# Split or unsplit key-value sums for two heads, a moved group of matmuls, and a split changed in one slot

## The chip, the cores and the metric

The kernel runs on one core of a Trainium2 chip. The metric is the device time of one launch in microseconds (us). Before the change three runs took 871.21, 871.63 and 871.66 us.

## What is computed

A linear attention, a mixture of experts with one expert per token, and a dense two-layer network, one behind the other, all in 32-bit floats:

```python
def phi(x):                                   # q, k, v: 4 batches x 8 heads x 576 tokens x 64
    proj = x @ w_phi                          # 64 -> 128
    proj = proj - max(abs(proj))              # of each row
    return concat([exp(proj), exp(-proj)])    # 256
kv, z = phi(k).T @ v, sum(phi(k))             # for each head
x = (phi(q) @ kv) / (phi(q) @ z + 1e-6)       # 2304 tokens x 512
e = argmax(normalised(x) @ normalised(expert_emb).T / tau)   # one of 8 experts
x = gate * (relu(x @ w1[e]) @ w2[e])          # 512 -> 1024 -> 512
h = x @ w_in                                  # 512 -> 2048
out = (h * sigmoid(h)) @ w_out                # 2048 -> 512
```

## The kernel before

**Split and unsplit products.** A float32 matrix product is made in one of two ways. Split: an operand is rounded to the faster fp32r format on ScalarE (`hi`), the remainder `lo` is subtracted on VectorE or GpSimd, and three matmuls (hi x hi, hi x lo, lo x hi) replace one. Unsplit: the float32 data go to TensorE as they are, in a slower form of matmul, and nothing need be rounded.

**The heads.** The loop over `g` from -2 to 31 (line 1478 and after) works at several heads at once. Within one pass, in the order of every engine's queue: `project(g + 3)` multiplies q and k of a head by w_phi on TensorE (line 402); `shift(g + 3)` takes the row maximum and subtracts it on VectorE (lines 411, 412; the second writes `d`); `kv_turn(g + 1)` turns the key-value sum (line 494, copied by VectorE in line 496); `numden(g)` makes numerators and denominators into the one tile `pnx` (lines 504, 509); `norm(g)` divides them on VectorE (lines 517 to 529); `qturn(g + 2)` transposes q (line 420); the exponentials of k of head g + 3 are taken on ScalarE; `kv_part(g + 2)` makes the key-value sum (line 481); `qexp(g + 2)` takes the exponentials of q; `high(g + 5)` and `low(g + 5)` round the next input z on ScalarE and subtract on GpSimd (lines 385, 391).

Where `g + 3 >= KWHOLE`, `kwhole` writes the two exponentials (line 445) and `kv_part` uses them unsplit with v. Otherwise `vhigh` and `vlow` split v (ScalarE line 424, GpSimd line 427), and `kexp`, `kround` and `klow` make each of the two exponentials (ScalarE line 437), round it (ScalarE line 449) and subtract (GpSimd line 453); `kv_part` then makes 15 fp32r matmuls. Before, KWHOLE is 26; heads 0 and 1 are unsplit too.

**The choice and the route.** Beside the heads VectorE converts packed weights of the last stage (`narrow`, lines 207 to 222, two steps in the passes of `BITS`). When a batch is done, `choose` picks each token's expert on VectorE (lines 534 to 555); for batch 2 all its steps are taken in the pass g = 24, in front of `norm(24)`. In the pass g = 25, `ranks` counts tokens per expert (lines 576 to 588 and 149 to 152). `route_first` is a generator that makes the token lists of the first six slots from batches 0 to 2; each `next(first)` takes a step. Its last step (lines 655 to 659) multiplies match matrices `bm` and `at` on TensorE into a free corner of the PSUM tile `pkv` of head 28, and VectorE copies and adds the result into the indices `gidx` and writes the expert registers `regs_a`. The tile tag of `pkv` has two buffers, so head 30 takes the buffer of head 28. Before, this last step stands in the pass g = 27, behind `kv_part(29)`, followed by `gather(0)` and `gather(1)`, which fetch the tokens of two slots with indirect DMAs from GpSimd (line 861). `load2(0)` on the SP queue reads `regs_a` in the pass g = 28. `xturn(0)` in the pass g = 29 transposes what `gather(0)` brought (line 901).

**The slots.** 22 slots of 128 tokens follow; slot s multiplies by w1 and w2 of its expert. `split(s, 2, i)` splits quarter i of w2 (lines 878 and 866, 1024 columns each; a quarter holds two half-blocks of 512). Of the last quarter `unsplit2(s)` half-blocks stay unsplit (line 893 instead of lines 826 to 828), and the matching part of the transposed activations is copied and not split (`halves`, lines 885 to 888). Before, two half-blocks are unsplit in slots 0 to 4 and one in slots 5 to 14 and 17.

The dense network follows in a form with seven products in place of eight; nothing of it is touched.

Of the kernel before, what the change touches and what calls it, by code (L numbers as in the profile page):

```python
# [20 lines left out]
B, H, S, D, F, E = 4, 8, 576, 64, 128, 8  # L21
# [18 lines left out]
HALF = (NSF - NP) // 2  # L40
POS = [2, 5, 1, 4, 0, 3] + [NP + i // 2 + HALF * (i % 2) for i in range(NSF - NP)]
SPLIT = NP + HALF
KWHOLE = 26
CA = 10
G = B * H
RK = 2
# [12 lines left out]


def unsplit2(s):
    return 2 if s < 5 else int(s < 15 or s == 17)

# [1 line left out]
def moe_kernel(ctx, tc, qk, v, w_phi, emb, tau, w1, w2, win, wout, out):  # L67
# [193 lines left out]
    def phase_all(ctx):  # L261
# [40 lines left out]
        def load_v(g):  # L302
            b, h = divmod(g, H)
            ve = ves[g % 4]
            nc.sync.dma_start(out=ve[:, 0:4, 0:64], in_=v[b, h, 0:512, :].rearrange("(c p) d -> p c d", p=P))
            nc.sync.dma_start(out=ve[others[1 - g % 2], 4, 0:64], in_=v[b, h, 512:S, :])
            st["v", g] = ve
# [86 lines left out]
        def whole(g):  # L394
            return g < 2 or g >= KWHOLE

# [8 lines left out]
        def shift(g, src=None):  # L405
            src = pqk if src is None else src
            n = chunks(g)
            pv = src[:, 0:n * 256].rearrange("p (n f) -> p n f", f=F)
            m = attA.tile([P, 2 * n], F32, name=f"m{n}")
            d = attA.tile([P, n, 2, F], F32, name=f"d{n}")  # L410
            nc.vector.tensor_reduce(out=m, in_=pv, axis=AX.X, op=ALU.max, apply_absolute_value=True)  # L411
            nc.vector.tensor_tensor(out=d.rearrange("p c s f -> p (c s) f"), in0=pv,  # L412
                                    in1=m.unsqueeze(2).to_broadcast([P, 2 * n, F]), op=ALU.subtract)
            st["d", g] = d
# [8 lines left out]
        def vhigh(g):  # L423
            nc.scalar.copy(out=vhs[g % 2][:, :, 0:64], in_=st["v", g][:, :, 0:64])

        def vlow(g):
            nc.gpsimd.tensor_tensor(out=vls[g % 2][:, :, 0:64], in0=st.pop(("v", g))[:, :, 0:64],
                                    in1=vhs[g % 2][:, :, 0:64].bitcast(F32), op=ALU.subtract)

        def kexp(g, s):  # L430
            kd = st["d", g][:, :, 1, :]
            n = chunks(g)
            if s == 0:
                st["k", g] = [pool.tile([P, n, 2, F], F32R, name=f"{nm}{n}", bufs=n - NB + 2)
                              for pool, nm in ((attA, "kl"), (attB, "kh"))]
            ke = attA.tile([P, NB, F], F32, name="ke", bufs=2)[:, 0:n]
            nc.scalar.activation(out=ke, in_=kd, func=AF.Exp, scale=1.0 - 2.0 * s)  # L437
            st["ke", g, s] = ke

        def kwhole(g):  # L440
            n = chunks(g)
            ke = attA.tile([P, n, 2, F], F32R, name=f"kl{n}", bufs=n - NB + 2).bitcast(F32)
            kd = st["d", g][:, :, 1, :]
            for s in range(2):
                nc.scalar.activation(out=ke[:, :, s, :], in_=kd, func=AF.Exp, scale=1.0 - 2.0 * s)
            st["k", g] = [ke]

        def kround(g, s):
            nc.scalar.copy(out=st["k", g][1][:, :, s, :], in_=st["ke", g, s])  # L449
# [142 lines left out]
        def matches(b):  # L592
            nc.vector.tensor_tensor(out=bm[:, b * NB:(b + 1) * NB], in0=jot.unsqueeze(1).to_broadcast([P, NB, P]),
                                    in1=lows.pop(b).unsqueeze(2).to_broadcast([P, NB, P]), op=ALU.is_equal)
# [262 lines left out]
        def gather(s):  # L857
            xg = mp.tile([P, DM], F32, tag="t2a", name="xg", bufs=3)
            n = (B - 1) * S if s < NP else NT
            p = POS[s]  # L860
            nc.gpsimd.indirect_dma_start(out=xg, out_offset=None, in_=xd[0:n, :],  # L861
                                         in_offset=bass.IndirectOffsetOnAxis(ap=gidx[:, p:p + 1], axis=0))
            st["xg", s] = xg
# [4 lines left out]
        def split(s, which, i, later=False):  # L868
            src = (raw1 if which == 1 else raw2)[s % 2].rearrange("p k f -> p (k f)")
            sl = src[:, i * 1024:(i + 1) * 1024]  # L870
            n = 1024
            if i == 3:
                n -= 1024 * unsplit1(s) if which == 1 else 512 * unsplit2(s)
            hi = lo = None
            if n:
                hi = wr.tile([P, 1024], F32R, tag=f"wh{which}", name=f"wh{which}", bufs=4)
                lo = wr.tile([P, 1024], F32R, tag=f"wl{which}", name=f"wl{which}", bufs=4)
                nc.scalar.copy(out=hi[:, 0:n], in_=sl[:, 0:n])  # L878
                if not later:
                    remainder(hi, lo, sl, n)  # L880
            st["w", which, s, i] = (hi, lo, sl, n)
            return lambda: remainder(hi, lo, sl, n)
# [14 lines left out]
        def xturn(s, early=False):  # L897
            xg = st.pop(("xg", s))
            pt = bank("xt", name="pxt")
            for k in range(4):  # L900
                nc.tensor.transpose(out=pt[:, k * P:(k + 1) * P], in_=xg[:, k * P:(k + 1) * P], identity=ident)  # L901
            xh = mp.tile([P, DM], F32R, name="xh")
            xl = mp.tile([P, DM], F32R, name="xl")
            xw = mp.tile([P, P], F32, name="xw")
            halves(pt, xh, xl, None if early else xw, DM - P * unsplit1(s))
            st["x", s] = (xh, xl, xw)
            return lambda: nc.scalar.copy(out=xw, in_=pt[:, DM - P:])
# [558 lines left out]
        first = None  # L1466
# [11 lines left out]
        for g in range(-2, G):  # L1478
# [11 lines left out]
            if g == G - H + 1:  # L1490
                first = route_first(r1)
# [2 lines left out]
                next(first)  # L1494
            if 2 <= g + 3 < G:
                shift(g + 3)
            if g == G - H + 2:
                next(first)
            if g == G - 1:
                xwhole = xturn(1, True)  # L1500
                wlast = split(1, 1, 2, True)
# [31 lines left out]
            if H <= g < G - H and h == RK:  # L1533
                ranks(b - 1, beside(g + 1))
                matches(b - 1)
            if KWHOLE <= g + 3 < G:
                kwhole(g + 3)
            if 3 <= g + 3 < KWHOLE:
                vhigh(g + 3)
                vlow(g + 3)  # L1540
            if 2 <= g + 3 < KWHOLE:
                kexp(g + 3, 0)
# [9 lines left out]
            for u in () if g == -2 else (3, 4) if g == -1 else (g + 5,):  # L1552
                if u < G:
                    load_v(u)
            if g == G - H + 3:
                next(first)
                gather(0)
                gather(1)
            if 2 <= g + 3 < KWHOLE:
                kround(g + 3, 1)  # L1560
                klow(g + 3, 1)
# [264 lines left out]
    with ExitStack() as c2:  # L1826
        phase_all(c2)
# [36 lines left out]
```

## Time and profile before

| | |
|---|---|
| profiled execution | 871.61 us |
| its span, first to last instruction | 870.0 us |
| mean granted clock of TensorE, share of full | 0.999 |
| TensorE (PE) busy | 857.8 us, 99% of the span |
| VectorE (DVE) busy | 703.1 us, 81% |
| ScalarE (ACT) busy | 609.7 us, 70% |
| GpSimd (POOL) busy | 269.2 us, 31% |

PE, DVE, ACT and POOL are the engines' names in the profile; PEld is TensorE's loading of the stationary operand, which overlaps PE; SP is the engine that issues most DMAs. A busy TensorE can still be one that waits in part of the time of a matmul, since ends of matmuls are modelled. Times in rows are in us from the start of the span, and "L402" is line 402 of the kernel.

### The profile page before, as it was taken

Reading aid. Unit: us, or ns where it says so; the run is one execution under the profiler, and the core shown is the slowest. Engines: PE = TensorE matmul, PEld = TensorE weight load, DVE = VectorE, ACT = ScalarE, POOL = GpSimd, SP = SyncE. Lnnn points to the kernel's source line nnn. Section 1 sums busy time; section 2 is a strip of 40 time slices with the busy share of each in tenths; the row PEclk is TensorE's granted clock in tenths of the full one; section 3 lists DMA queues with packets and bytes.
Section 4 is the critical chain, followed back from the end, with each engine's and each line's share of the span. In section 5 each row is a group of like instructions: output and inputs, shape, how many; then the busy total and the mean of one; then the engine's idle time right before and its main releaser. Section 6 shows DMA issues by size and latency. Waiting matters only on the chain. (4 is left out here: it accounts for less than half of the span.)

```text
span 870.0 us, 16082 instructions
## 1 busy us (share of the span) xinstructions
PE 857.8 (99%) x5730; PEld 786.8 (90%) x5730; DVE 703.1 (81%) x1112; ACT 609.7 (70%) x960; POOL 269.2 (31%) x261
## 2 busy tenths in 40 slices
PE   8999999999999999999999999999999999999996
PEld 6999999988777778888888899999999999999996
DVE  7888888897899999999998866666865797676762
ACT  6787888755977888888999866444546776556551
POOL 5888788721401533204220013032020101111011
PEclk9999999999999999999999999999999999999999
DMA  7445463439696696787599576588699944716221
GB/s 216 138 130 173 113 176 101 138 105 382 222 243 196 226 267 208 281 286 166 152 338 331 198 260 246 180 272 297 225 310 336 346 122 122 216 63 183 73 75 47
DMA packets 128805, 177.47 MB, mean 204 GB/s; under 512 B 26409, under 2 KB 89513, under 8 KB 128721
## 3 DMA queue, kind: packets, MB, share of 16 engines
q1 hardware_dynamic: 113888, 142.29, 50.4%
q0 software_dynamic: 14752, 34.09, 13.9%
q8 instruction: 46, 0.75, 0.4%
q14 instruction: 39, 0.31, 0.1%
q10 hardware_dynamic: 80, 0.03, 0.0%
HBM read 173.49 MB, written 55.18 MB: 263 GB/s over the span
## 5 line engine op out<-in xcount | busy, mean ns | idle before, releaser
L866 DVE TENSOR_TENSOR wl<-raw,wh 128x1024 fp32r<-128x1024 f32 (+1 forms) x166 | 190.1, 1184 | 16.9 <-ACT wh L878 11.0
L878 ACT CAST wh<-raw 128x1024 fp32r<-128x1024 f32 (+1 forms) x166 | 164.6, 1036 | 21.9 <-PE ph L828 7.4
L1137 ACT COPY ht<-puA 128x384 f32<-128x384 f32 x93 | 44.4, 479 | 79.3 <-PE puA L828 72.0
L453 POOL TENSOR_TENSOR kl<-ke,kh 128x640 fp32r<-128x640 f32 (+1 forms) x48 | 71.7, 1510 | 22.4 <-ACT kh L449 21.4
L826 PE MATMUL ph<-wh,xh 128*128 128x512 f32 x166 | 67.2, 405 | 0.0
L828 PE MATMUL ph<-wh,xl 128*128 128x512 f32 x166 | 65.1, 392 | 1.1 <-DVE xl L888 1.1
L827 PE MATMUL ph<-wl,xh 128*128 128x512 f32 x166 | 64.9, 391 | 0.0
L504 PE MATMUL pnx<-kv,qp 128*128 128x73 f32 x512 | 62.3, 275 | 0.0
L504 PEld LDWEIGHTS pnx<-kv,qp 128*128 128x128 f32 x512 | 59.9, 192 | 0.2
L411 DVE TENSOR_REDUCE m<-pqk 128x10 f32<-128x1280 f32 (+1 forms) x31 | 42.2, 1361 | 18.8 <-PE pqk L402 18.5
L402 PE MATMUL pqk<-wbd,zh 128*128 128x256 f32 x280 | 52.2, 285 | 0.5 <-DVE d L412 0.4
L437 ACT ACTIVATE ke<-d 128x640 f32<-128x640 f32 (+1 forms) x48 | 32.9, 685 | 26.9 <-DVE d L412 15.3
L861 POOL DMA_INDIRECT xg<-xd,gidx x22 | 29.5, 1343 | 70.9 <-PE pxt L901 30.0
L391 POOL TENSOR_TENSOR zl<-z,zh 128x640 fp32r<-128x640 f32 (+1 forms) x30 | 42.3, 1409 | 27.6 <-ACT zh L385 22.0
L1144 DVE TENSOR_TENSOR ht<-puC,ht 128x384 f32<-128x384 f32 x48 | 26.5, 553 | 30.0 <-PE puC L828 25.5
L402 PEld LDWEIGHTS pqk<-wbd,zh 128*128 128x128 f32 x280 | 43.1, 189 | 1.9 <-issue 1.2
L412 DVE TENSOR_TENSOR d<-pqk,m 128x1280 f32<-128x1280 f32 (+1 forms) x31 | 42.2, 1362 | 2.3 <-PE qt L420 1.2
L828 PE MATMUL pdA<-wod,hl 128*128 128x256 f32 x144 | 40.8, 284 | 0.0
L402 PE MATMUL pqk<-wbd,zl 128*128 128x256 f32 x140 | 39.4, 281 | 0.5 <-DVE zl L391 0.5
L828 PEld LDWEIGHTS ph<-wh,xl 128*128 128x128 f32 x166 | 31.2, 188 | 8.3 <-DVE xl L888 1.7
L1380 POOL DMA_INDIRECT out<-osd,oidx x10 | 12.9, 1289 | 81.6 <-ACT osd L1371 56.5
L461 ACT ACTIVATE qp<-qt 128x640 f32<-128x640 f32 (+1 forms) x64 | 37.8, 643 | 0.2 <-PE qt L420 0.2
(481 smaller groups left out, 2916.9 us busy)
## 6 DMA issues: line engine op xcount, KB each, us to landing
raw<-w SPq DMA_DIRECT2D x44, 1536.0 KB
raw<-w SPq DMA_DIRECT2D x44, 512.0 KB
hd<-ht SPq DMA_DIRECT2D x90, 192.0 KB
gb<-hd SPq DMA_DIRECT2D x18, 512.0 KB
ws<-wout SPq DMA_DIRECT2D x16, 512.0 KB
yd<-ys SPq DMA_DIRECT2D x22, 256.0 KB
z<-qk SPq DMA_DIRECT2D x16, 320.0 KB
raw<-win SPq DMA_DIRECT2D x10, 512.0 KB
```

Source lines behind the costliest of these rows:

```text
L391: eng.tensor_tensor(out=zl, in0=z, in1=zh.bitcast(F32), op=ALU.subtract)
L402: nc.tensor.matmul(out=to[:, c * 256:(c + 1) * 256], lhsT=z[:, c * P:(c + 1) * P], rhs=wbd[:, j].rearrange("p h f -> p (h f)"), start=(i = ...
L411: nc.vector.tensor_reduce(out=m, in_=pv, axis=AX.X, op=ALU.max, apply_absolute_value=True)
L412: nc.vector.tensor_tensor(out=d.rearrange("p c s f -> p (c s) f"), in0=pv, in1=m.unsqueeze(2).to_broadcast([P, 2 * n, F]), op=ALU.subtract)
L453: nc.gpsimd.tensor_tensor(out=kl[:, :, s, :], in0=st.pop(("ke", g, s)), in1=kh[:, :, s, :].bitcast(F32), op=ALU.subtract)
L504: nc.tensor.matmul(out=pn[:, c, 0:73], lhsT=qp[:, s, c * P:(c + 1) * P], rhs=kv[:, s, g % 2, 0:73], start=(s == 0), stop=(s == 1))
L826: nc.tensor.matmul(out=o, lhsT=ah, rhs=bh, start=first, stop=False, skip_group_check=more)
L827: nc.tensor.matmul(out=o, lhsT=ah, rhs=bl, start=False, stop=False, skip_group_check=more)
L828: return nc.tensor.matmul(out=o, lhsT=al, rhs=bh, start=False, stop=last, skip_group_check=more)
L866: nc.vector.tensor_tensor(out=lo[:, 0:n], in0=sl[:, 0:n], in1=hi[:, 0:n].bitcast(F32), op=ALU.subtract)
L878: nc.scalar.copy(out=hi[:, 0:n], in_=sl[:, 0:n])
L1137: nc.scalar.copy(out=htile(u, at), in_=BK[u, "A"])
```

## The change

Three edits. KWHOLE goes from 26 to 28, so heads 26 and 27 are split: in the passes g = 23 and 24 `vhigh`, `vlow`, `kexp`, `kround` and `klow` take the place of `kwhole`, and in the passes g = 24 and 25 `kv_part` has the split form. The last step of `route_first` and the two gathers move from the pass g = 27 to the pass g = 28, behind `project(31)` and `shift(31)`. And slot 5 has two unsplit half-blocks instead of one.

```diff
-KWHOLE = 26
+KWHOLE = 28
...
 def unsplit2(s):
-    return 2 if s < 5 else int(s < 15 or s == 17)
+    return 2 if s < 6 else int(s < 15 or s == 17)
...
             if 2 <= g + 3 < G:
                 shift(g + 3)
-            if g == G - H + 2:
+            if g in (G - H + 2, G - H + 4):
                 next(first)
+            if g == G - H + 4:
+                gather(0)
+                gather(1)
             if g == G - 1:
...
             for u in () if g == -2 else (3, 4) if g == -1 else (g + 5,):
                 if u < G:
                     load_v(u)
-            if g == G - H + 3:
-                next(first)
-                gather(0)
-                gather(1)
             if 2 <= g + 3 < KWHOLE:
```

G is 32 and H is 8, so G - H + 3 is 27 and G - H + 4 is 28.

## Rows read from the trace of the kernel before

**Rows 1.** The page, part 1: busy us, share of the span, instructions.

```profile
PE 857.8 (99%) x5730; PEld 786.8 (90%) x5730; DVE 703.1 (81%) x1112; ACT 609.7 (70%) x960; POOL 269.2 (31%) x261
```

**Rows 2.** The waits of VectorE, 172 to 208 us: total us, times, longest.

```profile
DVE m L411 <- PE pqk L402: 0.8, 1, 0.8
```

**Rows 3.** Timeline of TensorE: start us, us, engine, line, operation, out<-in, count.

```profile
170.01 0.36 PE L481 MATMUL pkv<-kh,vh 128*65 128x256 f32 x1
...
171.85 0.40 PE L402 MATMUL pqk<-wbd,zh 128*128 128x256 f32 x2
...
176.00 2.32 PE L481 MATMUL pkv<-kl,ve 128*65 128x256 f32 x10
177.97 0.58 PE L402 MATMUL pqk<-wbd,zh 128*128 128x256 f32 x2
...
180.63 1.95 PE L504 MATMUL pnx<-kv,qp 128*128 128x73 f32 x16
```

**Rows 4.** Timeline of VectorE, heads 25 and 27 and the pass g = 24.

```profile
162.12 1.22 DVE L412 TENSOR_TENSOR d<-pqk,m 128x1024 f32<-128x1024 f32 x1
...
164.44 1.27 DVE L222 SCALAR_TENSOR_TENSOR raw<-raw 128x512 int32<-128x512 int32 x1
...
174.73 1.22 DVE L412 TENSOR_TENSOR d<-pqk,m 128x1024 f32<-128x1024 f32 x1
...
178.82 0.69 DVE L222 SCALAR_TENSOR_TENSOR raw<-raw 128x512 int32<-128x512 int32 x1
...
179.94 0.42 DVE L522 TENSOR_TENSOR x<-pnx,rd 128x256 f32<-128x256 f32 x1
...
180.81 1.04 DVE L588 TENSOR_TENSOR rank<-rank,off 128x5 f32<-128x5 f32 x1
```

**Rows 5.** Timeline of GpSimd, the last split head and after.

```profile
165.12 2.97 POOL L453 TENSOR_TENSOR kl<-ke,kh 128x512 fp32r<-128x512 f32 x2
168.07 1.27 POOL L391 TENSOR_TENSOR zl<-z,zh 128x512 fp32r<-128x512 f32 x1
...
180.56 1.27 POOL L391 TENSOR_TENSOR zl<-z,zh 128x512 fp32r<-128x512 f32 x1 [4.93 <-ACT zh L385]
```

**Rows 6.** Timeline of all engines around the last projection, 197 to 211 us.

```profile
198.27 1.49 DVE L412 TENSOR_TENSOR d<-pqk,m 128x1280 f32<-128x1280 f32 x1
...
200.69 0.52 PE L655 MATMUL pkv<-at,bm 128*128 128x12 bf16 x15 [1.27 <-DVE at L650]
...
201.07 0.48 PE L402 MATMUL pqk<-wbd,zh 128*128 128x256 f32 x2
...
202.29 0.17 DVE L657 COPY pis<-pkv 128x12 f32<-128x12 f32 x1
...
202.77 1.23 DVE L411 TENSOR_REDUCE m<-pqk 128x8 f32<-128x1024 f32 x1
202.95 1.16 POOL L861 DMA_INDIRECT xg<-xd,gidx  x1 [7.15 <-DVE regs_a L659]
...
205.31 2.32 PE L481 MATMUL pkv<-kl,ve 128*65 128x256 f32 x10
...
210.15 0.60 PE L901 MATMUL pxt<-ident,xg 128*128 128x128 f32 x4
```

**Rows 7.** DMA issues of the whole span: operation, count, median us to landing.

```profile
xg<-xd,gidx POOLq DMA_INDIRECT x22, 5.6
```

**Rows 8.** Timeline of TensorE, end of slot 5's second product.

```profile
303.08 0.39 PE L826 MATMUL po<-wh,hh 128*128 128x512 f32 x1
...
303.76 1.02 PE L893 MATMUL po<-raw,hw 128*128 128x512 f32 x2
304.62 0.60 PE L934 MATMUL ht<-ident,hs 128*128 128x128 f32 x4
```

**Rows 9.** Timeline of TensorE, the first matmuls and a later group of the same.

```profile
1.27 3.95 PE L327 MATMUL qt<-ones 128*128 128x512 bf16 x10 [1.27 <-DVE ones L88]
...
9.31 1.69 PE L327 MATMUL pnx<-ones 128*128 128x512 bf16 x7
```

## The prediction

> **What bounds the kernel now.** I read the page's first part, then the waits of VectorE, then the timelines of the last heads, engine by engine. TensorE is busy for nearly the whole span [rows 1], so at first sight the only question is how much TensorE time the change removes. The waits of VectorE between 172 and 208 us tell another thing for the place where the change works: in these 36 us VectorE waited once, for 0.8 us, and that before 174 us [rows 2]. From then on it goes from one instruction to the next, because the choice of experts and the route are laid between the heads. TensorE and VectorE are both full there, and a delay of either is a delay of the end. After the heads the rest follows TensorE and ScalarE in a chain without slack, so I carry what is won or lost at the last heads to the end unchanged. The profiled execution took 871.61 us, 0.02 under the median of the three runs, so sums made in its rows need no correction.
>
> **Heads 26 and 27, TensorE.** The key-value sum of an unsplit head takes 1.97 us from its first matmul to the first of the projection behind it, that of a split head 1.84 [rows 3]. So the split saves 0.13 us a head, 0.26 for both, as an upper bound. It is worth nothing if VectorE sets the next step, and it does: the numerators of head 25 start at 180.63 [rows 3], right behind the normalisation of head 24, whose last part ends at 179.94 + 0.42 = 180.36 [rows 4], since both use the tile pnx. TensorE's margin over VectorE here is under 0.3 us. I count the saving as 0.
>
> **Heads 26 and 27, GpSimd against VectorE.** The split form adds for each head on ScalarE a rounding of v and two of the exponentials, and on GpSimd one subtraction for v and two for the exponentials. ScalarE has room; what its casts cost in delay is contained in the pattern that follows. Head 25, the last split one with an odd number, shows when GpSimd works: its shifted keys are ready at 162.12 + 1.22 = 163.34 [rows 4], its two key subtractions run from 165.12 to 168.09, and the subtraction of the next input z until 169.34 [rows 5]. That is 1.8 to 4.7 us and 4.7 to 6.0 us behind the keys. For head 27 the keys are ready at 174.73 + 1.22 = 175.95 [rows 4]. Laid behind them, the two key subtractions fill 177.7 to 180.7 and the one of z 180.7 to 182.0, where before GpSimd was idle until 180.56 [rows 5].
>
> In just this stretch VectorE has the choice of batch 2 (all nine steps at once, lines 534 to 555) and two bit operations (lines 220 and 222). What meets GpSimd is slow: line 222 takes 1.27 us at 164.44, where head 25's subtractions run beside it, and 0.69 at 178.82, where GpSimd is idle; and the 5-element operation of line 588 takes 1.04 us, ending with GpSimd's subtraction of z that began at 180.56 [rows 4, 5]. Such an operation, with two inputs in SBUF, ends only when GpSimd's does. Of the choice, lines 547 and 555 have this form. One meets the first key subtraction, the other the second, so line 555 ends at about 180.7. Line 220 follows in about the 0.69 of line 222, to 181.4, and line 222 meets the subtraction of z: 1.27 more, to 182.7. Before it ended at 178.82 + 0.69 = 179.51. **VectorE is 3.2 us later** at the normalisation of head 24, and TensorE, which waits for it, about 3.0 at the numerators of head 25. Then 0.87 comes back: line 588 no longer meets GpSimd and drops from 1.04 to about the 0.17 of another small operation [rows 6]. With VectorE full to the end of the heads [rows 2], 3.2 - 0.87 = 2.33 us remain. Bounds: nothing, if none of these operations meets GpSimd; and at most the two key subtractions and that of z waited for whole, 2.97 + 1.27 - 0.87 = 3.4. I take 2.33, because the same operations beside the same subtractions are in the trace.
>
> **The match products.** They leave TensorE's queue in front of the last projection, where they wait 1.27 us for line 650 [rows 6], and run behind it. The projection then starts when its bank is free, behind line 412 at 198.27 + 1.49 = 199.76, say at 199.9 instead of 201.07 [rows 6]: 1.2 us earlier. But little of this lasts. On VectorE the copy of the products (line 657) and the two operations behind it now stand behind the reduction and subtraction of head 31. These start at about 202.3 instead of 202.77, last 2 x 1.23, and end at 204.8; the copy of 0.17 ends at 204.97 [rows 6]. The products lie in the PSUM tile of head 28, and the key-value sum of head 30 takes that tile next. So this sum starts at about 205.05 instead of 205.31 [rows 6]: the gain shrinks to **0.26 us**. The upper bound is 1.27, if nothing else were late.
>
> Two gathers on GpSimd and the loads of the second weights on the SP queue stand behind the same indices and move by 204.8 - 202.3 = 2.5 us. The loads fill tiles that are first read after the last head; if that cover were gone they would cost up to 2.5. The gather of slot 0 was issued at 202.95, and its transposition started at 210.15 without a wait [rows 6]. Issued at 205.45 and wanted at 209.9, it has 4.4 us. The median landing of all gathers is 5.6 us [rows 7], so the wait is between 0 and 1.2 us; I take 0.2, as the DMA queues hold less at that time, the second weights not being asked for yet.
>
> **Slot 5.** One more half-block goes unsplit. An unsplit pair of matmuls takes 304.62 - 303.76 = 0.86 us, three split ones 303.76 - 303.08 = 0.68 [rows 8]: 0.18 us more on TensorE. ScalarE and VectorE lose a 512-column cast and subtraction. What that relieves is between 0 and the same 0.18; I take 0.
>
> **Sum:** 2.33 - 0.26 + 0.2 + 0.18 = +2.45 us, so 871.61 + 2.45 = **874.1 us**.
>
> **The rivals.** *Not slower: TensorE's account decides.* If GpSimd's subtractions fall between VectorE's operations instead of on them, VectorE is on time, and TensorE keeps 0.26 of the splits and between 0.26 and 1.27 of the match products, less 0.18: 870.3 to 871.3 us. For it speaks that VectorE's small operations take a small part of the stretch, and that GpSimd can only subtract what ScalarE has cast, so that a late cast leaves a gap for them; the point from which it decides is VectorE's margin of 0.3 us at the numerators of head 25. Against it speaks that GpSimd works through all of 177.7 to 182 without a hole. I give it 0.30, a third of that for a gain beyond 1.7 us with something freed in the slots.
>
> *Half of the collisions.* Line 222 starts before the subtraction of z, or line 555 before the second key subtraction, and the price falls by about 1.3 us: 872.8 us. Chance 0.20.
>
> *The clock falls.* TensorE would wait some 3 us in one place, more than twice the 1.27 of the trace [rows 6]. At the start, after idleness, ten matmuls of 512 columns took 3.95 us, 0.395 each; later seven took 1.69, 0.241 each [rows 9]: the levels of 1.2 and 2.4 GHz. One such start costs 10 x (0.395 - 0.241) = 1.5 us, so 875.6 us. The 1.27 us wait did not bring the clock down, as the mean granted clock of the span is nearly full (the table above), which says nothing of 3 us. The Trainium skill, "TensorE: Matmul & The Clock Gate", section on the HAM clock gate, says that the array's default is the lower clock and that idleness brings it back; by that rule the sum would be the 875.6 of this rival, by the rows it stays at 874.1. Chance 0.08.
>
> **The numbers.** The forecast itself has 0.42, with 873.4 to 875.2 as its own range. Changes under 0.2% (1.7 us) can hardly be told from none by a measurement of this kernel. Slower by more: the forecast and the clock, 0.50. Within: most of the first rival and the half collisions, 0.40. Faster: 0.10. The range of 8 in 10 takes in the first rival's lower end and the forecast's upper: 870.3 to 875.2.
>
> **What would show it.** In the changed trace: line 555 and line 222 of batch 2 ending with a GpSimd subtraction; a wait of 2.5 to 3.2 us of TensorE at line 504 for VectorE's normalisation; no wait at line 655; the key-value sum of head 30 starting with the end of line 657; the gather of slot 0 landing close to its transposition. I am wrong if the numerators of head 25 start within 0.5 us of 180.6, or if the last projection's 1.2 us are still there at the transposition of slot 0.

## The result, and the profile after

The changed kernel takes 879.11 us (median of five executions, 878.60 to 881.55) against 871.63: **7.5 us slower**, ratio 1.0083 with an interval of 1.0072 to 1.0094. The forecast was 874.1, the range ended at 875.2. The profiled execution after is the slowest of the five, 881.55 us with a span of 879.9, so its account ends 2.4 us above the median; where that lies is seen below.

The page's first part, changed kernel:

```profile
PE 862.2 (98%) x5739; PEld 790.6 (90%) x5739; DVE 704.4 (80%) x1111; ACT 612.7 (70%) x965; POOL 277.9 (32%) x267
```

TensorE is 4.4 us busier than in [rows 1], though the change gives it less to do at the heads. The waits of TensorE from 170 to 220 us (us in total, times, longest) say where to look:

```profile
PE pnx L504 <- DVE x L522: 2.3, 1, 2.3
PE pkv L611 <- DVE ohs L555: 0.6, 1, 0.6
PE pxt L901 <- DMA xg<-xd,gidx: 0.3, 1, 0.3
```

The wait at line 655 [rows 6] is gone, and a longer one stands at the numerators of head 25. The timeline of VectorE (start us, us, engine, line, operation) shows why the numerators wait; it answers to [rows 4]:

```profile
176.77 0.59 DVE L540 TENSOR_TENSOR lt<-lg,mx 128x40 f32<-128x40 f32 x1
...
177.64 0.20 DVE L545 TENSOR_REDUCE mx<-lt 128x5 f32<-128x40 f32 x1
177.87 0.96 DVE L547 TENSOR_TENSOR oh<-em8c,mx 128x40 bf16<-128x40 f32 x1
...
179.13 1.05 DVE L555 TENSOR_TENSOR ohs<-ohs 128x8 bf16<-128x8 bf16 x1
180.10 0.68 DVE L220 SCALAR_TENSOR_TENSOR raw<-raw 128x512 int32<-128x512 int32 x1
180.82 1.64 DVE L222 SCALAR_TENSOR_TENSOR raw<-raw 128x512 int32<-128x512 int32 x1
...
182.89 0.41 DVE L522 TENSOR_TENSOR x<-pnx,rd 128x256 f32<-128x256 f32 x1
...
183.67 0.16 DVE L588 TENSOR_TENSOR rank<-rank,off 128x5 f32<-128x5 f32 x1
```

The timeline of GpSimd over the same time answers to [rows 5]:

```profile
176.43 0.88 POOL L427 TENSOR_TENSOR vl<-ve,vh 128x320 fp32r<-128x320 f32 x1
177.41 2.75 POOL L453 TENSOR_TENSOR kl<-ke,kh 128x512 fp32r<-128x512 f32 x2
180.63 1.28 POOL L391 TENSOR_TENSOR zl<-z,zh 128x512 fp32r<-128x512 f32 x1 [0.46 <-PE pkv L582]
```

Lay the two side by side: line 540 ends with the subtraction of v, lines 547 and 555 with the first and the second key subtraction, each within 0.06 us. Line 555 works on 8 columns and takes 1.05 us. Line 222, of 512 columns, does not end with the subtraction of z but 0.55 us behind it (182.46 and 181.91). It did the same in the kernel before: what line 222 met at 164.44 [rows 4] was not a key subtraction but that of v, from GpSimd's timeline before:

```profile
163.83 1.34 POOL L427 TENSOR_TENSOR vl<-ve,vh 128x320 fp32r<-128x320 f32 x1
```

This one ended at 165.17, and line 222 at 165.71. The reduction of line 545 lies under the first key subtraction, too, and takes its 0.20 us all the same. The normalisation of head 24 ends at 183.30, 2.94 us later than before.

TensorE's timeline shows what the forecast had not counted; compare with [rows 3]:

```profile
180.23 0.17 PE L611 MATMUL pkv<-ohs,ones 128*128 128x8 bf16 x1 [0.60 <-DVE ohs L555]
...
183.35 3.69 PE L504 MATMUL pnx<-kv,qp 128*128 128x73 f32 x16 [2.27 <-DVE x L522]
...
190.99 0.40 PE L402 MATMUL pqk<-wbd,zh 128*128 128x256 f32 x2
```

The last row is the next projection, which in TensorE's timeline before starts here:

```profile
185.60 0.47 PE L402 MATMUL pqk<-wbd,zh 128*128 128x256 f32 x2
```

The numerators start 2.72 us late, and then the same 16 matmuls take 3.69 us where they took 1.95. From the numerators to the projection it is 7.64 us instead of 4.97. The windows of the changed kernel (stretch, length, busy us of PE, PEld, DVE, ACT and POOL, then the granted clock, the busy share of the DMA engines and GB/s) name the reason:

```profile
181.00:183.00 2.00, 0.08 (x1) 0.00 (x0) 1.93 (x5) 0.12 (x2) 0.91 (x1) 0.98 0.00 0
183.00:185.00 2.00, 1.65 (x8) 1.65 (x8) 1.83 (x9) 0.00 (x0) 0.00 (x0) 0.50 0.79 256
185.00:187.00 2.00, 2.00 (x11) 2.00 (x11) 1.97 (x2) 0.00 (x0) 0.00 (x0) 0.50 1.01 263
187.00:189.00 2.00, 2.00 (x11) 1.98 (x11) 1.43 (x6) 1.36 (x2) 0.00 (x0) 0.50 0.07 14
189.00:191.00 2.00, 2.00 (x16) 2.00 (x16) 0.86 (x5) 0.00 (x0) 0.00 (x0) 0.81 0.00 0
```

From 183 to nearly 190 us the granted clock is 0.50, the level of 1.2 GHz. TensorE is busy all that time, at half speed; this is where its busy time grew. The projection starts 5.4 us late.

Around the last projection all engines, in one timeline, against [rows 6]:

```profile
209.53 0.16 DVE L657 COPY pis<-pkv 128x12 f32<-128x12 f32 x1
...
209.74 2.37 PE L481 MATMUL pkv<-kl,ve 128*65 128x256 f32 x10
...
215.14 0.63 PE L901 MATMUL pxt<-ident,xg 128*128 128x128 f32 x4 [0.34 <-DMA xg<-xd,gidx]
```

The key-value sum of head 30 starts 0.05 us behind the end of line 657, and the gather of slot 0 lands 0.34 us too late, both as forecast. The transposition of slot 0 is 4.99 us later than before.

From there on I follow the first matmul of line 901 in each slot. The shifts against the kernel before, from the timelines of line 901 (span: its end), with the timed ratios of all runs. The column "early" has what the profile was shifted already at the key-value sum that starts at 99.81 us in the kernel before. No edit acts before 160 us, and from 20 to 170 us this shift stays the same, so it belongs to the execution and is to be taken off the columns to its right:

```
run                early   slot 0  slot 7  slot 10 slot 20  span   ratio  (interval)
changed            -0.05   +4.99   +5.04   +6.37   +8.16   +9.93  1.0083 (1.0072 to 1.0094)
e8_again           +0.09   +4.84   +4.86   +6.13   +6.95   +7.59  1.0080 (1.0062 to 1.0098)
e1_heads            0.00   +4.35   +4.34   +4.70   +4.70   +6.83  1.0075 (1.0054 to 1.0096)
e2_slot5            0.00   -0.01    0.00   +0.69   +1.69   +1.31  1.0008 (0.9996 to 1.0020)
e3_products        +0.47   +0.36   +0.37   -0.10   +2.13   +2.22  0.9996 (0.9983 to 1.0009)
e5_no_slot5        +0.31   +5.07   +5.08   +5.69   +5.69   +8.08  1.0070 (1.0050 to 1.0089)
e4_fill            +0.10   +1.88   +1.86   +3.29   +3.50   +4.33  1.0033 (1.0023 to 1.0044)
e6_bits_later      +0.04   +1.84   +1.85   +3.14   +3.42   +4.02  1.0056 (1.0035 to 1.0077)
e9_wait            -0.09   +1.32   +1.26   +1.09   +1.54   +2.13  1.0047 (1.0034 to 1.0060)
e10_wait_fill      +0.12   +1.58   +1.55   +2.50   +2.50   +3.89  1.0036 (1.0024 to 1.0047)
e14_wait15         +0.15   +5.06   +5.09   +5.05   +5.05   +5.28  1.0043 (1.0031 to 1.0056)
e15_wait15_fill     0.00   +1.98   +1.96   +2.14   +3.36   +4.92  1.0037 (1.0024 to 1.0050)
e11_k_later        +0.26   +3.15   +3.19   +4.02   +4.61   +5.77  1.0048 (1.0035 to 1.0061)
e12_k_later_slot5  +0.04   +2.72   +2.76   +3.04   +3.04   +5.30  1.0041 (1.0028 to 1.0053)
e13_z_later         0.00   -0.60   -0.66   -0.93   -0.93   -0.63  0.9980 (0.9966 to 0.9993)
e16_slot5_kept     +0.02   +4.45   +4.46   +5.53   +6.65   +8.29  1.0072 (1.0048 to 1.0096)
e17_slot5_whole    -0.17   +4.66   +4.66   +5.03   +5.03   +6.60  1.0058 (1.0040 to 1.0076)
```

One execution of e4_fill took 941.86 us at a mean granted clock of 0.851 and is not in its ratio.

The first line has four steps: 5.0 us at the heads, 1.3 between slots 7 and 10, 1.8 in front of slot 20, 1.8 behind it. The last three show in waits of TensorE behind the heads, changed kernel:

```profile
PE pt L1062 <- ACT xf L1068: 1.6, 1, 1.6
PE puA L826 <- ACT ht L1137: 0.9, 1, 0.9
PE py L828 <- DVE hl L888: 0.7, 1, 0.7
```

Slot 5 itself grew by the forecast 0.18: its end in TensorE's timeline has two unsplit pairs now, against [rows 8]:

```profile
308.12 1.88 PE L893 MATMUL po<-raw,hw 128*128 128x512 f32 x4
309.83 1.04 PE L934 MATMUL ht<-ident,hs 128*128 128x128 f32 x8
```

### The profile page after: what moved, and what is told of

Read it like the earlier page. It is cut to its first block, busy times and chain, and to the rows that moved or that the text cites. A ratio compares the mean times of both kernels' runs of the same rounds, so it can differ in the third digit from the quotient of the medians.

```text
span 879.9 us, 16111 instructions
## 1 busy us (share of the span) xinstructions
PE 862.2 (98%) x5739; PEld 790.6 (90%) x5739; DVE 704.4 (80%) x1111; ACT 612.7 (70%) x965; POOL 277.9 (32%) x267
## 5 line engine op out<-in xcount | busy, mean ns | idle before, releaser
L453 POOL TENSOR_TENSOR kl<-ke,kh 128x640 fp32r<-128x640 f32 (+1 forms) x52 | 77.5, 1507 | 24.2 <-ACT kh L449 22.8
L437 ACT ACTIVATE ke<-d 128x640 f32<-128x640 f32 (+1 forms) x52 | 35.6, 685 | 29.7 <-DVE d L412 16.1
```

What stands on the lines that cost most here:

```text
L453: nc.gpsimd.tensor_tensor(out=kl[:, :, s, :], in0=st.pop(("ke", g, s)), in1=kh[:, :, s, :].bitcast(F32), op=ALU.subtract)
```

## The experiments

My theory after this reading: VectorE's collisions with GpSimd make TensorE wait, the wait brings its clock down, and slot 5's edit does something to a load. The rivals: the loss sits in the moved products or in slot 5, or the clock falls for another reason.

**The parts one by one.** Only the heads (the kernel before with one line changed):

```diff
-KWHOLE = 26
+KWHOLE = 28
```

> Heads 26 and 27 split, nothing else changed. Theory: VectorE's choice and bit operations meet GpSimd's subtractions, TensorE then waits some 2.3 us at the numerators of head 25, and the granted clock falls to 0.5 for some 7 us behind that wait: +5 us at the end of the heads, which stay to the end, 876 to 877 us. Rival (no fall of the clock without the moved match products, the loss is the collisions alone): +2.3 us, 874 us. Second rival (the loss sits in slot 5 and in the moved products): under +1 us, 871.6 to 872.6 us.

Measured: 1.0075, 878.5 us where 876 to 877 was expected, +4.35 us at slot 0, the same two waits of 0.6 and 2.3 us, the clock at 0.50 between 183 and 187 us. The heads alone do most of it; both rivals fall. Which of the two heads does it was not measured: the kernel with head 26 alone split gave no time. The subtractions that collide in the rows above are all of the pass g = 24, which splits head 27.

Only slot 5:

```diff
-    return 2 if s < 5 else int(s < 15 or s == 17)
+    return 2 if s < 6 else int(s < 15 or s == 17)
```

> Two unsplit half-blocks in slot 5, nothing else changed. Theory: +0.2 us of matmuls in slot 5, and VectorE, with one subtraction less, frees the first weights' tile 0.7 us sooner; the next load goes out sooner and delays the load before it, so that TensorE waits some 1 us for VectorE in slot 6's second product: +1.4 us, 873.0 us. Rival (the wait in slot 6 of the changed kernel is only a shift that came from the late heads): +0.2 us, 871.8 us, and no wait in slot 6.

Measured: 1.0008, between the two. Nothing at the heads, +0.69 from slot 7 to slot 10, without the wait of 0.7 us for slot 6 that the theory asked for. Undecided; taken up again below.

Only the products and gathers (the changed kernel with KWHOLE = 26 and slot 5 as before):

> The match products and the first two gathers moved behind the last projection, nothing else changed. Theory: TensorE's wait at the products goes, the key-value sum of head 30 gains 0.26 us, the gather gives 0.2 to 0.4 back: between -0.3 and +0.3 us, 871.3 to 871.9 us. Rival (the late gathers and loads of the second weights cost more): +1 to +2.5 us, 872.6 to 874.1 us.

Measured: 0.9996, nothing that can be told from zero. In the profile +0.36 at slot 0, but this execution was 0.47 us late from its start. TensorE's timeline of this run, the last projection and the key-value sum of head 30:

```profile
200.37 0.48 PE L402 MATMUL pqk<-wbd,zh 128*128 128x256 f32 x2 [0.48 <-DVE d L412]
...
205.37 2.37 PE L481 MATMUL pkv<-kl,ve 128*65 128x256 f32 x10
```

Less 0.47 the projection starts at 199.90 instead of 201.07, the sum at 204.90 instead of 205.31 [rows 6], and slot 0 comes 0.1 us earlier than before: a gain, and a small one, as the theory has it. The wait in front of line 1062 is in this profile too, with 2.0 us, and it makes up nearly the whole of its later shift. Nothing near slot 17 was changed here: that wait comes and goes from one execution to the next, and the changed kernel's 1.6 us may be nothing else.

The changed kernel without slot 5's edit, and the changed kernel once more:

```diff
-    return 2 if s < 6 else int(s < 15 or s == 17)
+    return 2 if s < 5 else int(s < 15 or s == 17)
```

> The changed kernel with slot 5 as before (one unsplit half-block). Theory (slot 5's edit sends the load of slot 7's first weights out 0.7 us sooner, and the load before it lands later): +5.0 us at the transposition of slot 0, as in the changed kernel, no growth in slot 5, and at most 0.4 us more in slot 6; about 1.3 us below the changed kernel, ratio to before 1.0068. Rival (the late landing came from the late heads or by chance): the same 1.2 us in slot 6, and the time of the changed kernel less 0.2.

> The changed kernel once more, beside the three above. Theory: the collisions, the 2.27 us wait and the clock at 0.5 from about 183 to 190 us again, +5.0 us at the transposition of slot 0, and the wait of some 0.7 us in slot 6 again; the 1.6 us wait at the fetched rows behind slot 17 is not of the change and may be absent: ratio to before 1.007 to 1.010. Rival (these places differ from run to run): less than +3 us at slot 0 or no low clock.

Measured: +5.07 and +4.84 at slot 0, so the loss at the heads is nearly the same each time (5.04, 4.75 and 4.76 less the early shifts). From slot 7 to 10 the changed kernel lost 1.3 both times, without slot 5's edit 0.6. The ratios, 1.0070 and 1.0080, go the same way, with intervals that overlap.

**The clock.** The changed kernel, and TensorE busy where it waited. The columns written are free and nobody reads them:

```diff
+        qt_last = [None]
...
+            qt_last[0] = qt
...
+            if g == G - H + 1:
+                for _ in range(13):
+                    nc.tensor.matmul(out=qt_last[0][:, 640:1024].rearrange("p (a b) -> p a b", a=3), lhsT=ones,
+                                     rhs=ones.unsqueeze(1).to_broadcast([P, 3, P]), start=True, stop=True)
             if 0 <= g < G - 3:
                 numden(g)
```

> The changed kernel with 13 matmuls of 384 columns, which nothing reads, put in front of the numerators of head 25, so that TensorE works where it waited. Theory (the clock fell because of the wait): the granted clock stays at full behind them, the 2.7 us that the low clock cost are back: 876.4 us, the transposition of slot 0 at 212.5 instead of 215.1 us. Rival (the clock falls for another reason, or the time was lost otherwise): the same 879 us or more, with the clock at 0.5 from 183 to 190 us as before.

Measured: 1.0033, a median of 875.0 us. The windows of this run, in the stretch where the changed kernel had 0.50:

```profile
183.00:185.00 2.00, 1.83 (x16) 1.49 (x14) 1.83 (x10) 0.00 (x0) 0.00 (x0) 1.00 0.70 226
185.00:187.00 2.00, 2.00 (x19) 2.00 (x19) 1.97 (x2) 0.00 (x0) 0.00 (x0) 1.00 1.00 270
```

The clock stays at 1.00. VectorE is as late as before (its line 222 takes 1.65 us here), yet, less the early shifts, slot 0 comes 1.8 us late instead of 5.0: **the low clock cost some 3 us, the collisions 1.8.** The five profiles with the whole change at the heads and the low clock stand at 4.4 to 5.0 us, 2.7 to 3.3 above this one. Work that nobody needs made the kernel some 4 us faster.

The 3 us are of the profiled executions. Of the changed kernel's five, three have a mean granted clock of 0.993 to 0.995 and spans of 877.1 to 879.9 us; two have 0.997, as the kernel before has in some executions, and spans of 876.6 and 877.0. Half the clock for 6.8 us takes 0.004 from the mean, so these two may have had no such fall, and they are only a little faster.

The two bit operations behind the normalisation instead of in front of it:

```diff
-BITS = [-1, 0, 1, 2, 3, 4, 5, 6, 7, 11, 12, 13, 14, 15, 19, 20, 21, 22, 23, 24]
+BITS = [-1, 0, 1, 2, 3, 4, 5, 6, 7, 11, 12, 13, 14, 15, 19, 20, 21, 22, 23]
```

> The changed kernel with the two bit operations (lines 220 and 222) behind the normalisation of head 24 instead of in front of it. Theory (the wait of 2.27 us brought the clock down): the normalisation ends at about 181.0 us, the numerators of head 25 wait less than 0.3 us, the clock stays at full, and with the collisions still there the transposition of slot 0 is 1 to 2 us later than before instead of 5.0: about 3 us below the changed kernel, ratio to before 1.004 to 1.005. Rival (the clock falls from the 0.6 us wait in front of it or from the shorter matmuls): the clock at 0.5 for some 7 us there too, and +4 us or more at slot 0.

Measured: +1.84 at slot 0, and 1.0056, at the upper side of what was expected. The numerators wait for nothing; the one wait left in this stretch is 1.1 us at line 611, in front of 181 us, and the windows show a shorter fall:

```profile
181.00:183.00 2.00, 2.00 (x22) 1.86 (x18) 1.93 (x5) 0.20 (x2) 0.98 (x1) 0.93 0.00 0
183.00:185.00 2.00, 2.00 (x10) 2.00 (x10) 1.83 (x9) 0.00 (x0) 0.00 (x0) 0.50 0.38 117
185.00:187.00 2.00, 2.00 (x14) 1.98 (x14) 1.97 (x2) 0.00 (x0) 0.00 (x0) 0.72 0.99 286
```

So the expectation that the clock stays at full was wrong: here it fell behind a wait of 1.1 us, for half as long. It cost little at slot 0, where this run is no later than the one with the matmuls; VectorE, not TensorE, set the next steps.

Is it the wait alone? The kernel before, heads unsplit, with small copies on VectorE that nobody reads, ahead of the normalisation of head 24 (12 of them in the first pair, 15 in the second; the second run of each pair has 13 or 15 matmuls as above in front of the numerators):

```diff
+            if g == G - H:
+                pad = fin.tile([64, 8], F32, name="pad")
+                for _ in range(12):
+                    nc.vector.tensor_copy(out=pad, in_=pnx[0:64, 448:456])
             if g >= 0:
                 norm(g)
```

> The kernel before with 12 small copies on VectorE (8 columns each, read by nobody) in front of the normalisation of head 24, some 0.2 us each; heads 26 and 27 unsplit, the match products and slot 5 as before. Theory (a wait of TensorE alone brings the clock down): the numerators of head 25 wait some 2.2 us, the granted clock falls to 0.5 for up to 7 us; VectorE's own delay is 2.4 less the 0.9 of line 588, some 1.5 us, and the low clock adds 2 to 3: +3.5 to +4.5 us at the transposition of slot 0, ratio 1.004 to 1.0055. Rival (the split form's matmuls or the 0.6 us wait ahead of it are needed for the fall): the clock at full and +1.5 us, ratio 1.0017.

> The same 12 copies in the kernel before, and 13 matmuls of 384 columns, which nothing reads, in front of the numerators of head 25. Theory: the clock stays at full, +1.5 us at the transposition of slot 0, 2 to 3 us below the run without the matmuls, ratio 1.001 to 1.0025. Rival: the clock plays no part, and this run is not faster than the one without them.

Measured: a wait of 1.8 us, and in the profiled execution no fall, +1.41 at slot 0 less the early shift, as the +1.46 with the matmuls: where the clock does not fall, the matmuls change nothing. The profiled execution took 874.07 us; the other four took 875.35 to 877.67, three of them with a mean granted clock of 0.994 to 0.996 where the profiled one has 0.997. The pair does not decide whether a wait alone brings the clock down, so the wait was made as long as the changed kernel's:

> As the run with 12 copies in the kernel before, with 15: the numerators of head 25 wait some 2.35 us, as long as in the changed kernel. Theory (the wait alone brings the clock down, and at 1.8 us it did so in some executions only): the granted clock at 0.5 for several us behind the wait in the profiled run, mean clock 0.994 to 0.996 in all executions, +1.9 us of VectorE's delay and 2 to 3 us of low clock at the transposition of slot 0: ratio 1.005 to 1.0065. Rival (the split form's matmuls are needed): clock at full, +1.9 us, ratio 1.002 to 1.003.

> The same 15 copies, and 15 matmuls of 384 columns in front of the numerators of head 25. Theory: the clock at full, +1.9 to 2.3 us at the transposition of slot 0, mean clock 0.998, ratio 1.002 to 1.0035, 2 to 3 us below the run without the matmuls. Rival: as slow as that run.

Measured, TensorE's timeline with 15 copies and no matmuls:

```profile
183.30 3.05 PE L504 MATMUL pnx<-kv,qp 128*128 128x73 f32 x13 [2.37 <-DVE x L522]
```

The windows of the same run:

```profile
183.00:185.00 2.00, 1.70 (x8) 1.70 (x9) 1.83 (x9) 0.00 (x0) 0.00 (x0) 0.50 0.66 198
185.00:187.00 2.00, 2.00 (x11) 2.00 (x11) 1.97 (x2) 0.00 (x0) 0.00 (x0) 0.50 0.00 0
```

The windows of the run with the matmuls in the gap:

```profile
183.00:185.00 2.00, 2.00 (x19) 1.85 (x17) 1.83 (x9) 0.00 (x0) 0.00 (x0) 1.00 0.59 172
```

Less the early shifts +4.9 us at slot 0 against +2.0: some 3 us again, without split heads, moved products or slot 5. In this profile a wait of TensorE is enough. The timed ratios, 1.0043 and 1.0037, do not tell the two kernels apart: in two of the six executions without matmuls the mean clock is 0.996 and 0.997 and the time 875.35 and 874.85 (the others 876.9 to 877.1 at 0.994 and 0.995), so a low mean clock goes with some 2 us within this kernel, and the profile with matmuls loses 3.0 us behind slot 7, the other 0.2. What that is I leave open.

**The collisions.** The changed kernel, with head 27's two key subtractions behind the subtraction of z; below it the same with slot 5 as before:

```diff
                 kround(g + 3, 0)
-                klow(g + 3, 0)
+                if g != G - H:
+                    klow(g + 3, 0)
...
                 low(g + 5, nc.gpsimd)
+            if g == G - H:
+                klow(g + 3, 0)
+                klow(g + 3, 1)
```

> The changed kernel with the two key subtractions of head 27 behind the subtraction of the next z on GpSimd, so that they no longer lie under the choice of batch 2. Theory (the collisions are the cause of the late VectorE): lines 547 and 555 at 0.20 and 0.16 us, line 222 at 0.69, the wait at the numerators of head 25 under 0.8 us, the clock at full; some later small operation meets the moved subtractions, so the transposition of slot 0 is 0.3 to 1.3 us later than before instead of 5.0; with slot 5 and 6 +1.4: ratio 1.001 to 1.003. Rival (the split form is slow for another reason, ScalarE's casts or the sums themselves): +3 us or more at slot 0.

> The same with slot 5 as before: split heads 26 and 27 and moved products alone, without the collisions. Theory: the same +0.3 to +1.3 us at slot 0, no growth in slot 5 and at most 0.6 in slot 6, some 1 us below the run with slot 5 changed: ratio 1.000 to 1.002. Rival (slot 5's edit costs only its 0.2 us of matmuls, and slot 6 waits by chance): the same time as that run less 0.2.

Measured: VectorE's timeline of the first of the two:

```profile
178.17 0.20 DVE L547 TENSOR_TENSOR oh<-em8c,mx 128x40 bf16<-128x40 f32 x1
...
178.67 0.16 DVE L555 TENSOR_TENSOR ohs<-ohs 128x8 bf16<-128x8 bf16 x1
...
179.47 0.69 DVE L222 SCALAR_TENSOR_TENSOR raw<-raw 128x512 int32<-128x512 int32 x1
...
181.37 0.85 DVE L588 TENSOR_TENSOR rank<-rank,off 128x5 f32<-128x5 f32 x1
182.26 1.20 DVE L149 TENSOR_SCALAR rq<-rank 128x5 f32<-128x5 f32 x1
183.49 1.19 DVE L150 TENSOR_SCALAR rq<-rq 128x5 f32<-128x5 f32 x1
```

Lines 547, 555 and 222 are fast again, as expected, and the clock stays at full. But slot 0 is 2.9 and 2.7 us late (less the early shifts), not 0.3 to 1.3: line 540 still meets the subtraction of v, line 588 that of z, and the moved subtractions met lines 149 and 150, two that have a single input of 5 columns (1.20 us instead of 0.17). The collision does not go away, it moves. And TensorE waits 0.9 and 0.7 us for the gather of slot 0. So the rival's +3 us is nearly met in number, but its reason is not needed: lines 149 and 150 alone lose 2.05 us. TensorE waits nearly 3 us here, too, in four pieces of 0.4 to 1.05, and keeps its clock.

The same idea where it can work. In the kernel before, line 588 meets GpSimd's subtraction of z [rows 4, 5]. ScalarE squares three parts of batch 2 first and rounds that z afterwards, so that GpSimd is later:

```diff
+            if g == G - H:
+                for c in range(3):
+                    squares(b - 1, c, 0, 0, DM)
             if 5 <= g + 5 < G:
                 high(g + 5)
```

(the squares are taken out of their old places.)

> The kernel before with one collision less: in the pass of head 24 ScalarE squares three parts of batch 2 first and only then rounds the z of head 29, so that GpSimd's subtraction of it falls behind line 588, beside lines 411 and 412, which read PSUM. Theory: line 588 at 0.16 us instead of 1.04, VectorE 0.9 us earlier, and TensorE's wait at the match products shrinks from 1.27 to 0.4 to 0.9 us: 0 to 0.9 us faster, ratio 0.999 to 1.000. Rival (TensorE is full there, or the subtraction only meets another operation): 0, ratio 1.000, or slower if lines 411 and 412 are slowed.

Measured, all engines in one timeline:

```profile
180.81 0.17 DVE L588 TENSOR_TENSOR rank<-rank,off 128x5 f32<-128x5 f32 x1
...
181.57 1.48 DVE L411 TENSOR_REDUCE m<-pqk 128x10 f32<-128x1280 f32 x1
...
182.68 1.27 POOL L391 TENSOR_TENSOR zl<-z,zh 128x512 fp32r<-128x512 f32 x1 [7.05 <-ACT zh L385]
...
183.09 1.49 DVE L412 TENSOR_TENSOR d<-pqk,m 128x1280 f32<-128x1280 f32 x1
```

Line 588 takes 0.17, GpSimd's subtraction lies beside lines 411 and 412, and neither slows the other (1.48 and 1.49, as in [rows 6] and before). Slot 0 comes 0.60 us earlier, and the ratio is 0.9980 (0.9966 to 0.9993): this kernel **beats both**, with the one collision taken out instead of four put in. The timed gain is larger than expected: 871.25 us against 873.04 in the executions beside it, 1.8 us, of which the profile shows 0.6.

**Slot 5 and the load.** Between slots 7 and 10 TensorE waits for VectorE's hl of slot 6, VectorE for the cast of line 878, and that for the last load of slot 6's second weights. The trace's semaphore events complete this load 10.6 us behind the transposition of slot 7 in the kernel before and 12.0 in the changed one. The next loads go out sooner. The timeline of SP's queue, changed kernel:

```profile
308.11 0.47 SPq L839 DMA_DIRECT2D raw<-w  x2
```

The timeline of ScalarE, the cast that waits for the older load:

```profile
315.67 0.62 ACT L878 CAST wh<-raw 128x512 fp32r<-128x512 f32 x1 [5.35 <-PE ph L828]
```

The issue is 4.54 us behind the transposition of slot 7 (303.57), where it was 5.28. The reason that the code gives: VectorE has one subtraction of 512 columns less and frees the tile of slot 9's first weights sooner (the expectations call it slot 7's). The cast's row names TensorE, but of the things it waits for the load was the last before it, at 315.57. To move the issue alone, slot 5 still multiplies two half-blocks unsplit, but casts and subtracts as before, or, in the second run, a whole quarter; nobody reads it:

```diff
+            keep = which == 2 and s == 5 and i == 3
             if i == 3:
-                n -= 1024 * unsplit1(s) if which == 1 else 512 * unsplit2(s)
+                n -= 1024 * unsplit1(s) if which == 1 else 512 * (1 if keep else unsplit2(s))
...
-            st["w", which, s, i] = (hi, lo, sl, n)
+            st["w", which, s, i] = (hi, lo, sl, 0 if keep else n)
```

> The changed kernel, in which slot 5 still multiplies two half-blocks unsplit, but ScalarE's cast and VectorE's subtraction of the second one are done as before, and nobody reads them. Theory (the missing subtraction lets the next loads out sooner, and they hold up the last load of slot 6's second weights): those loads go out 5.3 us behind the transposition of slot 7, as before, not 4.55; the held-up load is complete 10.6 to 11.2 us behind it, not 11.9 to 12.1; slots 7 to 10 lose 0.2 to 0.7 us instead of 1.3; +5.0 us at slot 0 as in the changed kernel; ratio 1.007 to 1.008. Rival (the extra unsplit matmuls, or chance, make the load late): complete at 11.9 us or later, and 1.1 us or more lost from slot 7 to 10.

> As the run before, but the cast and the subtraction that nobody reads cover the whole last quarter of slot 5's second weights (1024 columns instead of 512), so that VectorE frees the next loads' tile some 0.5 us later still. Theory (the time at which the next loads go out decides): they go out 5.4 us or more behind the transposition of slot 7, the held-up load is complete 10.6 to 11.2 us behind it, slots 7 to 10 lose 0.2 to 0.7 us. Rival (the time at which they go out plays no part; the load is late with the extra unsplit matmuls or by chance): complete at 11.6 us or later and 1 us or more lost, though the next loads go out late.

Measured: the first came out in between, issue at 5.00, load complete at 11.7, 1.07 us lost between slots 7 and 10. The second goes past the kernel before; the timeline of SP's queue:

```profile
308.72 0.47 SPq L839 DMA_DIRECT2D raw<-w  x2
```

The timeline of ScalarE in this run, the same cast (the edit moved it one line down):

```profile
313.66 0.62 ACT L879 CAST wh<-raw 128x512 fp32r<-128x512 f32 x1 [3.72 <-DMA raw<-w]
```

Issue at 5.53, load complete at 10.4, 0.37 us lost, of which 0.18 are matmuls. Four issue times, 4.54, 5.00, 5.28 and 5.53, give 12.0, 11.7, 10.6 and 10.4. Over all profiles the load is complete at 10.4 to 11.2 where the issue is at 5.14 or later, and at 11.7 to 12.1 where it is at 5.00 or sooner, with one exception: where only slot 5 was changed the issue is at 4.55 and the load complete at 11.0. So the extra unsplit matmuls do not make it late, and it goes with the time of the issue, but not in every execution; why it is delayed no run shows. The loss from slot 7 to 10 varies, too: the six profiles with slot 5's edit as it is have 0.69 to 1.43 us (1.14 on average), the nine without it -0.47 to +0.95 (0.16). The ratio, 1.0058, lies below the changed kernel's two, with intervals that overlap.

## Why the prediction was wrong

**Splits, TensorE.** Counted at nothing, and right: VectorE set the step.

**GpSimd against VectorE.** Right in its mechanism and nearly in size. Line 222 ends at 182.46 (forecast 182.7), the numerators start 2.72 us late (3.0), line 588 gives its time back (0.16), and what is left at slot 0 without the clock is 1.8 us; with the other steps the forecast had 2.3 there. Line 540 had not been expected to collide, and line 222 took 1.64, not the 1.27 of the trace before. The rule "ends only when GpSimd's does" holds for the small operations; line 222 ended 0.55 us behind GpSimd's in both traces, so its price depends on where it starts. That it ends so near to the forecast is in part luck: the key subtractions ended 0.5 us sooner (180.16, not 180.7), and line 222 took 0.4 longer.

**The clock: the step that failed.** The sum has no term for it. "The clock falls" was a rival with a chance of 0.08, and its price was 1.5 us, taken from ten matmuls at the start of the kernel. The chance was too low and the price half of what was measured. The clock fell in all six profiles in which the numerators of head 25 waited 2.27 us, and it cost some 3 us. The chance rested on a wait of 1.27 us that did not bring the clock down, and the text said itself that this tells nothing of a wait of 3 us; with the mechanism of the forecast holding, the wait came with it, so the rival was no rival but the forecast's next step. The price is had from the work behind the wait: the 16 numerators take 3.69 us instead of 1.95, and all from them to the next projection 7.64 instead of 4.97, 2.7 us more. The Trainium skill, "TensorE: Matmul & The Clock Gate", section on the HAM clock gate, has idleness bring the lower clock back; the traces agree, with 0.50 granted from waits of 2.27 and 2.37 us on.

**Match products and gather.** Right. Forecast -0.26 and +0.2, measured together -0.1 (products alone, +0.36 less the 0.47 by which that execution was late from its start), and nothing in the timed ratio. The projection starts at 199.90 as forecast, the sum of head 30 stands behind line 657 and gains 0.4.

**Slot 5.** The 0.18 of matmuls was right. "What that relieves is between 0 and the same 0.18" bounded the effect on one side only: with the edit the profiles lose 1.0 us more from slot 7 to 10, 0.8 of it beyond the matmuls, and the late load is the likely way. In the timed runs this does not stand clear of the noise.

**The rest.** 5.0 + 1.3 makes 6.3 of the 7.5 us. The execution that is the median, 879.11 us, has a span of 876.6, which is 6.6 above the 870.0 of the profile before: in it 0.3 us of the remainder lie inside the span and 0.9 outside, before the first or behind the last instruction. In the profiled execution more lies behind slot 17, in waits at lines 1062 and 826 for ScalarE. The first is also in a kernel that changed nothing there, and the timed runs of the kernel before spread from 870.75 to 878.17 us over all comparisons. Whether the last 1 us belongs to the change I leave open.

## What to carry to other kernels

When a forecast says that TensorE will wait long in one piece in the middle of dense work (2.3 us here), the wait is not the end of the account: price the matmuls behind it at the lower clock, too, and if the wait can't be removed, matmuls that nobody reads can stand in it. Work given to GpSimd is not free in a stretch that VectorE fills with small element-wise operations on SBUF; put it beside VectorE's long operations that read PSUM. Relieving an engine can let loads go sooner, so look at which load is in flight at that moment, and who waits for it.

## What was not expected of the hardware

An operation on 8 columns takes 1.05 us when a GpSimd subtraction runs, and so does one with a single input of 5 columns (1.20 instead of 0.17). The Trainium skill, "SBUF — State Buffer", section "Who interferes with whom", says that VectorE with two inputs in SBUF, or in certain modes of copies and one-input operations, and GpSimd share a pair of ports which one of them holds for its whole instruction while the other is blocked; the runs agree: the slow operations of 5 to 40 columns end within 0.06 us of GpSimd's, those of 512 columns 0.55 us behind it, and reductions (line 545, 0.20 us) are not slowed. GpSimd is held up in turn: its subtraction of v takes 1.34 us at 163.83 in the kernel before, where line 220 was running, and 0.88 at 176.43 in the changed one.

Waits of the same size did not always have the same effect on the clock: a wait of 1.8 us was followed by no fall in one profiled execution, one of 1.1 us by a short fall in another kernel, and 1.27 us at line 655 by none.

Where the next loads went out 0.7 us sooner than before, an older load was complete 1.2 to 1.5 us later in five of six profiles, and 0.4 later in the sixth.
